# A fused spectral filter, router and expert kernel: where four groups of loads, three groups of spectra products and the narrowing of the last matrix stand in each engine's order

## The chip, the core and the metric

One Trainium2 chip, one of its cores. The metric is the device time of one launch in microseconds (us). The engines are TensorE (PE), VectorE (DVE), ScalarE (ACT), GpSimd (POOL) and SyncE (SP); each works through its own list of instructions in order and waits for the others by semaphores. SP, ACT and POOL also issue transfers.

## What is computed

The reference chains three parts. Only the batches that hold the first tokens matter in the usual case, since each expert takes the first tokens that choose it, up to a capacity.

```python
X = np.fft.rfft(x, axis=1)                      # x: 4 batches x 3072 x 256
Yr = Xr @ w_r - Xi @ w_i + b_r                  # Yi likewise; then soft threshold by 0.01
y = np.fft.irfft(Y, n=x.shape[1], axis=1)
...
logits = x @ w_gate                             # 8 experts, 384 places each, first come
h = np.maximum(np.einsum('ecd,edf->ecf', disp, w1), 0.0)
out[i] = gate_w[i] * y[expert_idx[i], pos[i]]   # y: h times w2
...
h = x @ w_in
return (h / (1.0 + np.exp(-h))) @ w_out         # 256 -> 2048 -> 256
```

## The kernel before

Large products are split into a high and a low part and done as three matmuls each (`mm3`, lines 205, 206 and 207). The transform is done as small transforms in stages. For a batch, `s1` or `first` is the first stage, `kphase` goes over 24 pairs of frequencies in steps of two (k = 0, 2, ... 22): `forward` makes `xp` (line 436) and splits it into `xk`, `shrink` makes the products `yp` with the spectral weights, 24 matmuls for a step (the "spectra products"), DVE thresholds them in three operations (lines 476 to 479), and `back` turns them back (`bp`, line 485), copies them to `bo` on ACT and stores them to DRAM as `b_d` in groups of four. The third stage is `is2`: for each of eight groups it loads rows `br` of `b_d` (two transfers, line 634), multiplies (`tiled`, line 361), copies the result to `ao` on ACT, stores it as `attn` from ACT's queue (line 640), transposes it (`tp`), copies it to `aT` on DVE and makes the logits `lg` (line 661). After four groups the logits are transposed (`lt`, line 668) and `choose` finds each token's expert on DVE.

`route` gives every token its place: a running count on DVE, matmuls `bs` (lines 695 to 698), a chain of small DVE operations, masks `pm` and `ft`, and the matmuls `tb` (line 753) that add to a table. `rank` and `slots` then read off which rows each expert takes; `gather` fetches them with indirect transfers on POOL (`xg`, three for an expert), `turn` scales them on DVE and transposes them (`gtp`, line 1064) into `xT`, and `first_ffn` runs one expert: `hp`, `hh` on ACT, `hl` on DVE (line 1087), `y`. Experts 0, 1 and 2 run first, with batch 1's third stage (`third`, line 575) and its routing beside them; then pairs of experts go through the last two matrices (`second_ffn`), which fill the last 340 us.

The two last matrices come as 64-bit floats and are narrowed on the chip. `narrow` loads a piece (`nt`), takes the absolute value on ACT (line 867), and runs four DVE operations (lines 868, 872, 873, 874); the caller then splits the result on ACT and POOL. `ffn_in` does `w_in` in eight pieces, four of them beside the first stage of batch 1 and four beside the third stage of batch 0. `ffn_out` does `w_out` in eight pieces, drawn from the loop over the experts: `n` counts that loop's steps (nine for each of experts 0, 1, 2), and at each step named in `AHEAD` one piece is written.

The order on each engine is not the order of the code. A scheduler with a timeline of its own writes each engine's list; `after(a, b)` tells it to place `a` behind `b`, without adding a wait on the chip. The tail of `kphase` for batch 1 is written behind `route`, so its products may be placed wherever the scheduler finds room; `PACE` ties some of its `xp` to steps of `is2`.

Of the kernel before, what the change touches and what calls it, by code (L numbers as in the profile page):

```python
# [26 lines left out]
QB, GT = 32, 8  # L27
# [7 lines left out]
MID = 0.5 * (P - 1)  # L35
EARLY = 3
WARM = 11
AHEAD = 4, 8, 12, 16, 20
PMS = "vav"
RING = 2  # L40
LATE = 3
PACE = {4: 2, 5: 5, **{n: GT - 1 for n in range(6, 12)}}
BIG = 65536.0
UP = 65536.0
F_MIN = UP * float(np.array(0x38000000, np.uint32).view(np.float32))
# [108 lines left out]
class Kernel:  # L154
    def __init__(self, ctx, tc, i, o):
        self.tc, self.nc, self.i, self.o = tc, tc.nc, i, o
        nc = self.nc
        cst = ctx.enter_context(tc.tile_pool(name="cst", bufs=1))
        self.dr = ctx.enter_context(tc.tile_pool(name="dr", bufs=1, space=bass.MemoryType.DRAM))
        self.zt = cst.tile([P, 1, D], F32, name="zt")  # L160
        nc.vector.memset(self.zt, 0.0)
        self.ident = cst.tile([P, P], F32, name="ident")
        make_identity(nc, self.ident)
        self.table = cst.tile([P, NF, SC * E], F32, name="table")
        self.carry = cst.tile([P, E], F32, name="carry")
        nc.gpsimd.memset(self.carry, 0.0)
        nc.gpsimd.memset(self.table, 0.0)
        self.attn = [self.dr.tile([n, D], F32, name=f"attn{h}") for h, n in enumerate((NEAR, NT - NEAR))]
        self.cst = cst
        self.tail = cst.tile([P, SC, 2, D], F32, name="tail")  # L170
        self.mixed = self.dr.tile([DFF // D, P, 3, P], F32, name="mixed")
        self.zeroed = 0
        self.stored, self.fetched, self.spread = {}, None, None
        self.again, self.away, self.evicted, self.gated = False, False, None, {}

    def spare(self, n, nm):

# [177 lines left out]
    def tiled(self, table, rows, pool):  # L355

        out = [pool.tile([P, self.CH], F32, tag="ps", name="ps1") for _ in range(2)]
        for ch in range(2):
            for p in range(2):
                at = slice(64 * p, 64 * p + N1)  # L360
                self.nc.tensor.matmul(out[p][64 * ch:64 * ch + 64], table[at, :64], rows[at, ch * self.CH:(ch + 1) * self.CH],
                                      start=True, stop=True)
        return out

    def first(self):
# [44 lines left out]
    def kphase(self, b, ads, ahead=False):  # L410

        nc, kp = self.nc, self.kp
        v = nc.vector
# [50 lines left out]
        def shrink(k, xk, xo):  # L464
            yp = self.pk.tile([P, 2, D], F32, tag="yq" if k % 4 and (b != 1 or k > 12) else "yp", name="yp", bufs=1)
            for j in range(2):
                for jj in range(2):
                    for c in range(2):
                        if jj and xo is not None and not j:
                            l = [xo[:, h, c] for h in range(2)]  # L470
                        else:
                            l = [xk[:, h, 2 * j + c, 64 - 64 * jj:192 - 64 * jj] for h in range(2)]
                        self.mm3(yp[:, j], l[0], l[1], wri[:, jj, 0, c], wri[:, jj, 1, c], jj + c == 0, jj + c == 2)
            y = self.spare(1, "y")
            bias = self.bias if xo is not None else self.bias[:, 1:2].to_broadcast([P, 2, D])
            v.tensor_tensor(y, yp, bias, ALU.add)  # L476
            cl = kp.tile([P, 2, D], F32, tag="cl", name="cl", bufs=3)
            v.tensor_scalar(cl, y, LAM, -LAM, ALU.min, ALU.max)
            self.shrunk = v.tensor_tensor(cl, y, cl, ALU.subtract).ins
            return cl  # L480
# [9 lines left out]
        x, y = {}, {}  # L490
# [122 lines left out]
    def is2(self, b, qbs, res):  # L613

        nc, bp, ps, wg = self.nc, self.bp, self.ps, self.wg
        v = nc.vector
        NB = len(qbs)  # L620
        T = QB // 2
        t0, nt = qbs[0] * T, NB * T
        bv = self.bds[b].rearrange("k (r p u g) c -> p (k r) u g c", r=2, p=2, u=4)
        r0 = b * S + t0 * 2 * TW
        h = int(r0 >= NEAR)
        od = self.attn[h][r0 - h * NEAR:r0 - h * NEAR + nt * 2 * TW].rearrange("(t p u g) d -> t p u g d", p=2, u=4, g=GT)
        res[b] = self.chosen(NB)
        GS = 4
        lgs = {}

        def rows(g):
            br = bp.tile([P, 4, D], F32, tag="xt", name="br", bufs=self.sb)
            for p in range(2):
                nc.sync.dma_start(out=br[64 * p:64 * p + N1], in_=bv[p, :, :, g])
            pt = self.tiled(self.c4, br.rearrange("q u c -> q (u c)"), ps)
            ao = bp.tile([P, 2, 2, D], F32, tag="ao", name="ao2", bufs=self.sb)
            for p in range(2):
                nc.scalar.copy(ao[:, p].rearrange("q u c -> q (u c)"), pt[p])
            for ch in range(2):
                nc.scalar.dma_start(out=od[:, :, 2 * ch:2 * ch + 2, g], in_=ao[64 * ch + t0:64 * ch + t0 + nt])  # L640
            return ao

        def turn(ao):
            aT = bp.tile([P, 2, NB, P], F32, tag="aT", name="aT")
            for h in range(2):
                tp = ps.tile([P, 4, P], F32, tag="ps", name="tp")
                for x in range(4):
                    nc.tensor.transpose(tp[:, x], ao[:, x % 2, x // 2, h * P:(h + 1) * P], self.ident)
                for ch in range(2):
                    v.tensor_copy(aT[:, h].rearrange("c b (o x t) -> c o b x t", o=2, x=4)[:, ch],  # L650
                                  tp.rearrange("c x (o b t) -> c o b x t", o=2, t=T)[:, ch, qbs[0]:qbs[0] + NB])
            return aT

        def gate(g, aT):
            z = g % GS
            if not z:
                lgs[0] = self.pk.tile([P, GS, P], F32, tag="yq", name="lg", bufs=1)
            lg = lgs[0]
            for h in range(2):
                for j in range(NB):  # L660
                    self.gated[g] = nc.tensor.matmul(lg[COL * j:COL * (j + 1), z], wg[:, h], aT[:, h, j], start=h == 0, stop=h == 1).ins
            if z == GS - 1:
                n = COL * NB
                ls = self.spare(2, "ls").rearrange("p a (b c) -> p (a b) c", b=2)
                nc.scalar.copy(ls[:n], lg[:n])
                lt = ps.tile([P, GS, NB, COL], F32, tag="ps", name="lt")
                for y in range(GS):
                    nc.tensor.transpose(lt[:, y].rearrange("p b e -> p (b e)"), ls[:n, y], self.ident[:n, :n])
                self.choose(lt.rearrange("p g b e -> p b g e")[:, :, :, :E], res[b], slice(g + 1 - GS, g + 1))

        ao, aT = {}, {}
        for g in range(GT + 2):
            if g < GT:
                ao[g] = rows(g)
            if 0 < g <= GT:
                aT[g - 1] = turn(ao.pop(g - 1))
            if g > 1:
                gate(g - 2, aT.pop(g - 2))
            yield

    def route(self, b, qbs, res):
# [13 lines left out]
        nc.tensor.matmul(bs[:, 0], tri, last, start=True, stop=NB == 1)  # L695
        for j in range(1, NB):
            nc.tensor.matmul(bs[:, 0, :, j:], ones, last[:, :, :NB - j], start=False, stop=j == NB - 1)
        nc.tensor.matmul(bs[:, 1], ones, last, start=True, stop=True)
        v.tensor_tensor(inc, inc, oh, ALU.mult)
        ex = bp.tile([P, NC, 1], F32, tag="ex", name="ex", bufs=1)  # L700
        nc.gpsimd.tensor_scalar(ex, m2.rearrange("p b g o -> p (b g) o"), -1.0 * STEP, E * STEP - MID, ALU.mult, ALU.add)
# [31 lines left out]
        for j in range(NB):  # L733
# [16 lines left out]
                        self.after(here.ins, prev.ins)  # L750
                        self.made = here.ins
            for t in range(GT):
                nc.tensor.matmul(tb, pm[:, t], ft[:, j * GT + t], start=(j + t == 0), stop=(j * GT + t == NC - 1))
        for j in range(NB):
            v.tensor_tensor(self.carry, self.carry, bs[:, 1, :, j], ALU.add)
        v.tensor_tensor(self.table, self.table, tb, ALU.add)
# [96 lines left out]
    def narrow(self, src, n, after):  # L853
# [5 lines left out]
        t = pool.tile([P, n, 2], I32, tag="nt", name="nt", bufs=3)  # L859
        for sv, dv in src:  # L860
            ins = nc.sync.dma_start(out=t[:, dv], in_=sv.bitcast(I32).rearrange("p (n z) -> p n z", z=2))
            self.after(ins.ins, self.fetched)
        low, high = t[:, :, 0], t[:, :, 1].bitcast(F32)
        a = pool.tile([P, n], F32, tag="na", name="na")
        u = a.bitcast(I32)
# [147 lines left out]
    def weights(self, s, later=0):  # L1013
# [11 lines left out]
        def quarter(z, behind=None):  # L1025
            for m, sv in enumerate((v1[:, :, z * D:(z + 1) * D], v2[:, 2 * z:2 * z + 2])):
                st = self.mq.tile([P, 2, D], F32, tag="st", name="st", bufs=4)
                nc.sync.dma_start(out=st, in_=sv)
                w = self.mq.tile([P, 2, 2, D], FR, tag=f"w{m}", name=f"w{m}")
                self.hi("a", w[:, 0], st)  # L1030
                if behind:
                    self.after(self.lastact.ins, behind)
                self.lo("p" if m and s < EARLY and not self.again else "v", w[:, 1], st, w[:, 0])
                out[m].append(w)

        for z in range(4 - later):
# [287 lines left out]
```

## Time and profile before

| | |
|---|---|
| device time, median of 3 runs | 625.69 us (625.66 to 627.39) |
| the profiled execution | 631.12 us, span 629.3 us, mean granted clock 0.985 |
| busy in the span | PE 604.0 us (96%), DVE 420.3, ACT 340.0, POOL 202.5 |

The profiled execution is 5.4 us longer than the median. PE is busy nearly all the time, so the table says little about where time can be won. What helps is a list of the places where PE waits, and of the stretches in which its granted clock is below 1.00. From about 285 us on, the two kernels' lists are the same work in the same order; only a branch that isn't taken differs.

### The profile page before, as it was taken

What the parts mean: (1) busy time and instruction counts of PE and PEld (TensorE: products, weight loads), DVE (VectorE), ACT (ScalarE), POOL (GpSimd) and SP (SyncE); (2) the same over time, 40 slices, a digit from 0 to 9 for tenths busy, and PEclk for the clock granted to TensorE, in tenths of its full rate; (3) what the DMA queues carried; (4) which work ended last, traced back from release to release, by engine and by line L of the source; (5) the groups of instructions that cost most, each with busy time, mean ns of one, the idle gap of its engine ahead of it and who ended that gap; (6) DMA issues with size and microseconds to landing.
All of it is one profiled execution on the core that took longest, in us unless ns stands there. A gap on an engine that the chain in (4) does not pass through costs nothing.

```text
span 629.3 us, 11503 instructions
## 1 busy us (share of the span) xinstructions
PE 604.0 (96%) x4128; PEld 562.8 (89%) x4128; DVE 420.3 (67%) x837; ACT 340.0 (54%) x722; POOL 202.5 (32%) x196
## 2 busy tenths in 40 slices
PE   9999999899989999899999999999999999999993
PEld 9888898567987688789999999999999999999993
DVE  2454878635973689889886687576577577485552
ACT  2535656344533556257775566556567555475561
POOL 1000113300044334254754503445403443163433
PEclk9999999999997999799999999999999999999998
DMA  8638867983446688610453543413433130010001
GB/s 205 195 98 248 286 212 236 266 232 86 168 145 215 185 255 269 204 51 26 131 179 119 157 137 110 153 33 118 142 125 110 50 126 24 14 63 27 15 2 55
DMA packets 66011, 86.09 MB, mean 137 GB/s; under 512 B 6068, under 2 KB 55864, under 8 KB 65944
## 3 DMA queue, kind: packets, MB, share of 16 engines
q1 hardware_dynamic: 53976, 69.53, 36.4%
q10 hardware_dynamic: 9664, 9.44, 4.8%
q0 software_dynamic: 2304, 6.29, 3.2%
q8 instruction: 34, 0.56, 0.4%
q14 instruction: 33, 0.27, 0.1%
HBM read 54.31 MB, written 30.93 MB: 135 GB/s over the span
## 4 chain that ended last, share of the span: by engine, by line
PE 85%; DMA 5%; DVE 5%; issue 2%; POOL 1%; ACT 1%; SPq 1%; POOLq 0%; DVEq 0%
PE o L206 7%; PE o L207 7%; PE o L205 7%; PE h L205 6%; PE h L206 6%; PE h L207 6%; PE hp L205 3%; PE hp L206 3%; PE hp L207 3%; PE y L207 3%; PE y L205 3%; PE y L206 3%; PE xp L436 3%; PE yp L205 3%; PE yp L207 3%; PE yp L206 3%
## 5 line engine op out<-in xcount | busy, mean ns | idle before, releaser
L1219 DVE TENSOR_TENSOR u<-h,u 128x384 f32<-128x384 f32 x224 | 117.6, 552 | 58.5 <-PE h L207 52.5
L1157 ACT ACTIVATE u<-u 128x384 f32<-128x384 f32 x128 | 64.2, 522 | 73.3 <-DVE u L1219 72.7
L206 PE MATMUL o<-wo,gl 128*128 128x256 f32 x369 | 99.8, 282 | 0.6 <-DVE gl L197 0.6
L207 PE MATMUL o<-wo,gh 128*128 128x256 f32 x369 | 99.8, 282 | 0.0
L205 PE MATMUL o<-wo,gh 128*128 128x256 f32 x369 | 88.0, 282 | 0.1
L197 POOL TENSOR_TENSOR ring<-mt,ring 128x384 fp32r<-128x384 f32 x32 | 37.9, 1184 | 135.7 <-ACT ring L189 135.7
L197 POOL TENSOR_TENSOR gl<-u,gh 128x384 fp32r<-128x384 f32 x62 | 65.1, 1067 | 29.1 <-ACT gh L189 26.4
L206 PEld LDWEIGHTS o<-wo,gl 128*128 128x128 f32 x369 | 69.7, 189 | 1.2 <-DVE gl L197 0.9
L207 PEld LDWEIGHTS o<-wo,gh 128*128 128x128 f32 x369 | 69.6, 189 | 0.0
L205 PEld LDWEIGHTS o<-wo,gh 128*128 128x128 f32 x369 | 65.3, 189 | 0.4 <-ACT gh L189 0.4
L189 ACT CAST gh<-u 128x384 fp32r<-128x384 f32 x126 | 63.2, 510 | 3.3 <-PE o L207 1.6
L1086 ACT ACTIVATE hh<-hp 128x384 fp32r<-128x384 f32 x64 | 31.4, 490 | 51.7 <-PE y L206 24.4
L1087 DVE SCALAR_TENSOR_TENSOR hl<-hp,hh 128x384 fp32r<-128x384 f32 x64 | 35.2, 554 | 33.2 <-ACT hh L1086 28.9
L205 PE MATMUL yp<-wri,xk 128*128 128x256 f32 x188 | 56.1, 298 | 0.9 <-DVE tail L476 0.9
L206 PE MATMUL yp<-wri,xk 128*128 128x256 f32 x188 | 53.9, 287 | 0.0
L207 PE MATMUL yp<-wri,xk 128*128 128x256 f32 x188 | 53.7, 286 | 0.0
L197 DVE TENSOR_TENSOR w<-st,w 128x512 fp32r<-128x512 f32 x52 | 38.1, 743 | 18.9 <-ACT w L189 18.1
L189 ACT CAST w<-st 128x512 fp32r<-128x512 f32 x64 | 38.7, 620 | 17.6 <-DMA st<-in_moe_w 9.1
L205 PE MATMUL hp<-xT,w 128*128 128x384 f32 x128 | 45.1, 353 | 1.5 <-DVE xT L197 1.5
L206 PE MATMUL hp<-xT,w 128*128 128x384 f32 x128 | 44.5, 347 | 0.0
L207 PE MATMUL hp<-xT,w 128*128 128x384 f32 x128 | 43.9, 345 | 0.0
L205 PE MATMUL y<-hh,w 128*128 128x384 f32 x128 | 43.9, 343 | 0.0
(254 smaller groups left out, 1512.0 us busy)
## 6 DMA issues: line engine op xcount, KB each, us to landing
st<-in_moe_w SPq DMA_DIRECT2D x64, 256.0 KB, 3.0
out<-zt SPq DMA_DIRECT2D x48, 256.0 KB, 3.4
b_d<-bo ACTq DMA_DIRECT2D x12, 512.0 KB, 4.1
mt<-mixed SPq DMA_DIRECT2D x32, 192.0 KB, 2.3
xt<-in_x SPq DMA_DIRECT2D x15, 384.0 KB, 7.0
nt<-in_moe_w_in SPq DMA_DIRECT2D x8, 512.0 KB, 5.2
nt<-in_moe_w_out SPq DMA_DIRECT2D x16, 256.0 KB, 5.3
a_d<-ao SPq DMA_DIRECT2D x8, 384.0 KB, 3.8
```

The source lines that it names most:

```text
L189: self.lastact = self.nc.scalar.copy(dst, src)
L197: return e.tensor_tensor(dst, src, raw(hi), ALU.subtract).ins
L205: first = nc.tensor.matmul(out, lh, rh, start=start, stop=False)
L206: nc.tensor.matmul(out, ll, rh, start=False, stop=False)
L207: return first.ins, nc.tensor.matmul(out, lh, rl, start=False, stop=stop).ins
L436: return [nc.tensor.matmul(xp[:, c], ar[:, kq, c * P:(c + 1) * P], c2[:, tb], start=True, stop=True).ins for c in range(2)]
L1086: self.rectified = nc.scalar.activation(hh, hp, AF.Relu).ins
L1087: self.evicted = nc.vector.scalar_tensor_tensor(hl, hp, 0.0, raw(hh), ALU.max, ALU.subtract).ins
L1157: act.activation(sg, sg, AF.Silu)
L1219: v.tensor_tensor(to, h, u, ALU.add)
```

## The change

Five edits. `narrow` places its loads behind the first matmul of the first `tiled` (`begun`) instead of behind the last load of the spectrum. The first products `yp` of steps k = 10, 14 and 18 of batch 1 are placed behind the last `lt`, `bs` and `tb` of the routing (`HOLD`). `AHEAD` names steps 2, 5, 8, 11 and 14 instead of 4, 8, 12, 16 and 20. The first low part of expert 0's second weight goes to DVE instead of POOL.

```diff
-AHEAD = 4, 8, 12, 16, 20
+AHEAD = 2, 5, 8, 11, 14
...
+HOLD = {10: "lt", 14: "bs", 18: "tb"}
...
-                self.nc.tensor.matmul(out[p][64 * ch:64 * ch + 64], table[at, :64], rows[at, ch * self.CH:(ch + 1) * self.CH],
-                                      start=True, stop=True)
+                ins = self.nc.tensor.matmul(out[p][64 * ch:64 * ch + 64], table[at, :64], rows[at, ch * self.CH:(ch + 1) * self.CH],
+                                            start=True, stop=True).ins
+                self.begun = self.begun or ins
...
+                        if b == 1 and k in HOLD and not jj and not c:
+                            self.after(ins, self.held[HOLD[k]])
...
-            self.after(ins.ins, self.fetched)
+            self.after(ins.ins, self.begun or self.fetched)
...
-                self.lo("p" if m and s < EARLY and not self.again else "v", w[:, 1], st, w[:, 0])
+                self.lo("p" if m and 0 < s + z and s < EARLY and not self.again else "v", w[:, 1], st, w[:, 0])
```

On SP, at the end of batch 0's spectrum, the list before is as follows (`nt` are the narrowing's loads of `w_in`, `ar` rows of batch 1, `br` the rows of the third stage):

```order
L861 DMA nt_1196<-in_moe2_w_in 128x1024
L861 DMA nt_1259<-in_moe2_w_in 128x1024
L420 DMA ar_1671<-a_d1_428 128x4x256
L861 DMA nt_1349<-in_moe2_w_in 128x1024
L861 DMA nt_1381<-in_moe2_w_in 128x1024
L420 DMA ar_1761<-a_d1_428 128x4x256
L909 DMA mixed_74<-mt_1270 128x2x384
L634 DMA br_1047<-b_d0_233 48x4x256 x2
L634 DMA br_1061<-b_d0_233 48x4x256 x2
L634 DMA br_1090<-b_d0_233 48x4x256 x2
```

The list of the change at the same place:

```order
L422 DMA ar_1671<-a_d1_428 128x4x256
L422 DMA ar_1761<-a_d1_428 128x4x256
L638 DMA br_1047<-b_d0_233 48x4x256 x2
L638 DMA br_1061<-b_d0_233 48x4x256 x2
L638 DMA br_1090<-b_d0_233 48x4x256 x2
L866 DMA nt_1196<-in_moe2_w_in 128x1024
L866 DMA nt_1259<-in_moe2_w_in 128x1024
L638 DMA br_1126<-b_d0_233 48x4x256 x2
L638 DMA br_1161<-b_d0_233 48x4x256 x2
L866 DMA nt_1349<-in_moe2_w_in 128x1024
L866 DMA nt_1381<-in_moe2_w_in 128x1024
L638 DMA br_1207<-b_d0_233 48x4x256 x2
```

The four loads have moved from ahead of the first `br` to behind the sixth and the tenth. On ACT the narrowing moves with them; the change has this at the start of the third stage (`ps1` is the result of the first matmuls, `na` the narrowing):

```order
L642 COPY ao2_1056<-ps1_1050 128x512
L190 COPY bo_1666<-bp_1712 128x512
L872 ACTIVATE na_1198<-nt_1196 128x512
L492 DMA b_d1_1019<-bo_1666 128x4x256
L642 COPY ao2_1056<-ps1_1051 128x512
L642 COPY ao2_1070<-ps1_1064 128x512
L644 DMA attn0_71<-ao2_1056 96x2x256 x2
L190 CAST wi_86<-na_1198 128x2x128
L872 ACTIVATE na_1261<-nt_1259 128x512
L190 CAST wi_86<-mt_1270 128x2x128
L642 COPY ao2_1070<-ps1_1065 128x512
```

A narrowing now stands between the two halves of one group's copy. On PE, at batch 0's routing, the list before has these rows; products `yp` are shown by the first row of a step and of what comes next (1817 is step k = 12, then 14, 16, 18, 20):

```order
L668 MATMUL lt_1407<-ident_62,tail_73 128x96 x4
...
L205 MATMUL yp_1817<-wri_228,xk_1763 128x256
...
L205 MATMUL yp_1863<-wri_228,xk_1807 128x256
...
L695 MATMUL bs_1425<-inc_1423,rt_1039 128x24
...
L205 MATMUL yp_1907<-wri_228,xk_1853 128x256
...
L205 MATMUL yp_1953<-wri_228,xk_1897 128x256
...
L205 MATMUL yp_1997<-wri_228,xk_1943 128x256
L753 MATMUL tb_1459<-ft_1453,pm_1460 128x72 x8
L753 MATMUL tb_1459<-ft_1453,pm_1470 128x72 x8
L753 MATMUL tb_1459<-ft_1453,pm_1488 128x72 x8
L206 MATMUL yp_1997<-wri_228,xk_1943 128x256
```

And the change:

```order
L672 MATMUL lt_1407<-ident_62,tail_73 128x96 x4
L206 MATMUL yp_1773<-wri_228,xk_1717 128x256
...
L700 MATMUL bs_1425<-inc_1423,rt_1039 128x24
...
L206 MATMUL yp_1817<-wri_228,xk_1763 128x256
...
L206 MATMUL yp_1907<-wri_228,xk_1853 128x256
...
L758 MATMUL tb_1459<-ft_1453,pm_1460 128x72 x8
L758 MATMUL tb_1459<-ft_1453,pm_1470 128x72 x8
L758 MATMUL tb_1459<-ft_1453,pm_1488 128x72 x8
...
L206 MATMUL yp_1953<-wri_228,xk_1897 128x256
...
L206 MATMUL yp_1997<-wri_228,xk_1943 128x256
```

Before, `tb` stands behind all but 47 of the 288 product matmuls of batch 1; now 72 are behind it. Between the last `lt` and `bs` there were 46, now 24. On DVE, at the end of expert 1, the list before mixes the fifth narrowing (`na_2946`, `nsg_3190`) with the sums of a pair of experts (`tm`, `yf`):

```order
L1087 SCALAR_TENSOR_TENSOR hl_2934<-hp_2926,hh_2933 128x384
L868 TENSOR_SCALAR na_2946<-na_2946 128x512
L1115 TENSOR_TENSOR tm_3071<-yf_2910,yf_2588 128x384
L873 SCALAR_TENSOR_TENSOR na_2946<-na_2946,nsg_2949 128x512
L1116 TENSOR_TENSOR tm_3072<-yf_2910,tm_3071 128x384
L699 TENSOR_TENSOR inc_2665<-inc_2665,oh_2185 128x64
L712 SCALAR_TENSOR_TENSOR base_2683<-bs_2667,carry_68 128x8
L1118 TENSOR_TENSOR yf_2910<-yf_2910 128x384
L874 SCALAR_TENSOR_TENSOR na_2946<-nt_2943,na_2946 128x512
L872 TENSOR_SCALAR nsg_3190<-nt_3184 128x512
L1121 TENSOR_TENSOR yf_2588<-yf_2588,tm_3072 128x384
L703 TENSOR_REDUCE pos_2673<-inc_2665 128x8
```

In the change the same stretch is:

```order
L1092 SCALAR_TENSOR_TENSOR hl_2946<-hp_2938,hh_2945 128x384
L1120 TENSOR_TENSOR tm_3071<-yf_2922,yf_2600 128x384
L696 SCALAR_TENSOR_TENSOR inc_2677<-smask_1036,oh_2185 128x64
L712 RECIPROCAL gt_2689<-sm_2187 128x8
L1121 TENSOR_TENSOR tm_3072<-yf_2922,tm_3071 128x384
L1123 TENSOR_TENSOR yf_2922<-yf_2922 128x384
L192 CAST gh_2691<-gt_2689 128x8
L1126 TENSOR_TENSOR yf_2600<-yf_2600,tm_3072 128x384
L198 TENSOR_TENSOR gl_2692<-gt_2689,gh_2691 128x8
L1092 SCALAR_TENSOR_TENSOR hl_2963<-hp_2955,hh_2962 128x384
```

The three operations of the fifth narrowing and the first (`nsg_3190`) of the sixth are gone from here; the fifth is now written at step 14 of the loop over the experts, where it was at step 20.

## Rows read from the trace of the kernel before

**Rows 1.** PE's waits, 80 to 300 us: us in total, times, longest.
```profile
PE gtp L1064 <- DVE xg L1057: 3.3, 2, 1.9
PE y L207 <- DVE hl L1087: 2.9, 1, 2.9
PE ps L361 <- DMA br<-b_d: 2.2, 1, 2.2
PE hp L205 <- DVE xT L197: 1.5, 1, 1.5
PE yp L205 <- DVE tail L476: 0.9, 1, 0.9
```

**Rows 2.** Four stretches: busy time of each engine, PE's clock, DMA share, GB/s.
```profile
193.03:251.24 58.21, 56.44 (x321) 46.38 (x320) 39.78 (x80) 32.52 (x65) 21.27 (x19) 0.96 0.75 228
116.18:150.10 33.92, 33.92 (x281) 21.12 (x281) 15.30 (x46) 13.56 (x26) 2.15 (x2) 1.00 0.77 211
190.67:197.08 6.41, 6.22 (x18) 5.49 (x19) 1.75 (x4) 1.45 (x3) 3.00 (x3) 0.50 0.60 193
258.60:265.20 6.60, 5.89 (x18) 5.89 (x19) 5.56 (x20) 0.98 (x2) 0.00 (x0) 0.50 0.83 261
```

**Rows 3.** The chain that ended last: start, us, piece.
```profile
86.71 0.87 PE bp L485 x4
...
105.56 7.43 DMA b_d<-bo
...
113.06 2.98 DMA br<-b_d
...
197.37 2.59 PE pw L1069 x12
```

**Rows 4.** SP's queue at the start of the third stage: start, us.
```profile
113.06 2.81 SPq L634 DMA_DIRECT2D br<-b_d  x6
```

**Rows 5.** The page's transfers: count, KB each, median us to landing.
```profile
b_d<-bo ACTq DMA_DIRECT2D x12, 512.0 KB, 4.1
...
nt<-in_moe_w_in SPq DMA_DIRECT2D x8, 512.0 KB, 5.2
```

**Rows 6.** ACT's waits, 84 to 165 us.
```profile
ACT na L867 <- DMA nt<-in_moe_w_in: 3.3, 3, 2.4
...
ACT wi L189 <- DVE na L874: 1.6, 2, 1.4
```

**Rows 7.** ACT's timeline: a narrowing, and a copy of one tile.
```profile
96.96 0.69 ACT L867 ACTIVATE na<-nt 128x512 f32<-128x512 f32 x1 [2.40 <-DMA nt<-in_moe_w_in]
...
114.00 0.59 ACT L189 COPY bo<-bp 128x512 f32<-128x512 f32 x1 [0.51 <-PE bp L485]
```

**Rows 8.** PE's timeline: first and last of 24 product matmuls, and `tb`.
```profile
105.09 0.36 PE L205 MATMUL yp<-wri,xk 128*128 128x256 f32 x1
...
107.93 0.28 PE L207 MATMUL yp<-wri,xk 128*128 128x256 f32 x1
...
175.50 2.77 PE L753 MATMUL tb<-ft,pm 128*128 128x72 f32 x24
```

**Rows 9.** DVE's timeline: the first and the third gathered tile.
```profile
185.42 0.35 DVE L1057 TENSOR_SCALAR xg<-xg,gws 128x256 f32<-128x256 f32 x1
...
189.40 1.41 DVE L1057 TENSOR_SCALAR xg<-xg,gws 128x256 f32<-128x256 f32 x1 [0.92 <-DMA xg<-attn,srcs]
```

**Rows 10.** DVE's timeline around the narrowing beside the experts.
```profile
243.85 1.67 DVE L874 SCALAR_TENSOR_TENSOR na<-nt,na 128x512 int32<-128x512 int32 x1
...
251.71 1.06 DVE L868 TENSOR_SCALAR na<-na 128x512 f32<-128x512 f32 x1
...
253.15 0.68 DVE L873 SCALAR_TENSOR_TENSOR na<-na,nsg 128x512 int32<-128x512 int32 x1
...
254.90 0.68 DVE L874 SCALAR_TENSOR_TENSOR na<-nt,na 128x512 int32<-128x512 int32 x1
255.50 1.50 DVE L872 TENSOR_SCALAR nsg<-nt 128x512 int32<-128x512 int32 x1
...
258.71 1.01 DVE L1087 SCALAR_TENSOR_TENSOR hl<-hp,hh 128x384 fp32r<-128x384 f32 x2
```

More of the change, by code (lines that the diff above doesn't have):

```diff
@@ L173, in __init__ @@
         self.stored, self.fetched, self.spread = {}, None, None
-        self.again, self.away, self.evicted, self.gated = False, False, None, {}
+        self.again, self.away, self.evicted, self.gated, self.begun, self.held = False, False, None, {}, None, {}
     def spare(self, n, nm):
@@ L472, in shrink @@
                             l = [xk[:, h, 2 * j + c, 64 - 64 * jj:192 - 64 * jj] for h in range(2)]
-                        self.mm3(yp[:, j], l[0], l[1], wri[:, jj, 0, c], wri[:, jj, 1, c], jj + c == 0, jj + c == 2)
+                        ins = self.mm3(yp[:, j], l[0], l[1], wri[:, jj, 0, c], wri[:, jj, 1, c], jj + c == 0, jj + c == 2)[0]
+                        if b == 1 and k in HOLD and not jj and not c:
+                            self.after(ins, self.held[HOLD[k]])
             y = self.spare(1, "y")
@@ L667, in gate @@
                 for y in range(GS):
-                    nc.tensor.transpose(lt[:, y].rearrange("p b e -> p (b e)"), ls[:n, y], self.ident[:n, :n])
+                    ins = nc.tensor.transpose(lt[:, y].rearrange("p b e -> p (b e)"), ls[:n, y], self.ident[:n, :n]).ins
+                self.held["lt"] = ins
                 self.choose(lt.rearrange("p g b e -> p b g e")[:, :, :, :E], res[b], slice(g + 1 - GS, g + 1))
@@ L697, in route @@
             nc.tensor.matmul(bs[:, 0, :, j:], ones, last[:, :, :NB - j], start=False, stop=j == NB - 1)
-        nc.tensor.matmul(bs[:, 1], ones, last, start=True, stop=True)
+        self.held["bs"] = nc.tensor.matmul(bs[:, 1], ones, last, start=True, stop=True).ins
         v.tensor_tensor(inc, inc, oh, ALU.mult)
@@ L752, in route @@
             for t in range(GT):
-                nc.tensor.matmul(tb, pm[:, t], ft[:, j * GT + t], start=(j + t == 0), stop=(j * GT + t == NC - 1))
+                self.held["tb"] = nc.tensor.matmul(tb, pm[:, t], ft[:, j * GT + t], start=(j + t == 0), stop=(j * GT + t == NC - 1)).ins
         for j in range(NB):
```

## The prediction

> **What bounds the kernel now.** PE is busy 96% of the span, so its list of work sets the time, and that list is the same before and after. The change can only move the places where PE stands still or runs at a low clock. I read the views in this order. First PE's waits between 80 and 300 us [rows 1]: five lines, and behind each the engine or the transfer that ended it. Then stretches by granted clock [rows 2]: after two of the waits a stretch stands at 0.50, which is the lower of the two levels, 1.2 against 2.4 GHz. It took 6.41 us at the end of the routing and 6.60 us between experts 1 and 2. Work at half the clock takes twice as long, so half of each is lost: 3.2 and 3.3 us. That makes three places:
>
> - A, where batch 0's spectrum ends: 2.2 us for `br`, 0.9 us for `tail`, together 3.1.
> - B, behind the routing: two waits of `gtp` for gathered tiles, 3.3 us, and 3.2 of clock, together 6.5.
> - C, from expert 1 to expert 2: 1.5 for `xT`, 2.9 for `hl`, 3.3 of clock, together 7.7.
>
> So 17.3 us can be won at most, and each place is judged by what else its stretch holds.
>
> **A: the loads behind the first matmul.** The chain that ended last runs through this place [rows 3]: the store `b_d` takes 7.43 us, `br` 2.98, and then PE goes on. The page has 4.1 us as the median of such a store [rows 5]. Here `nt` loads stand ahead on SP and share the DMA engines with it. Moved behind the sixth `br`, they leave the store alone: 7.43 - 4.1 = 3.3 us sooner, more than the 2.2 waited. The narrowing's DVE work leaves the stretch too, which is what kept `tail` (0.9). I take all 3.1.
>
> It is paid in the third stage, where the four loads and narrowings now stand. SP needs 2.81 us to issue six `br` [rows 4]; then `nt` starts and lands 5.2 us later [rows 5], 8.0 behind the first `br`, while that one lands after 2.98. ACT's list has the first narrowing behind two copies only, so ACT waits some 2 us, and the second half of the first group's copy `ao` waits behind it: 0.69 for the narrowing, 0.59 for a copy [rows 7]. PE has products between the groups, but the transposes wait for `ao`. Upper bound: the four loads are 2.1 MB; the stretch moved 211 GB/s at a DMA share of 0.77 [rows 2], so 274 at a full one, and 2.1 MB take 7.7 us; ACT's waits in narrowings are 4.9 us before (3.3 + 1.6) [rows 6]. If all were passed to PE, 12.6. Lower bound nothing: the stretch from 116 to 150 has ACT busy 13.56 and DVE 15.30 of 33.92 us [rows 2], room enough for the work of four narrowings. I take 2.7, a little over half of ACT's waits, since the products that stand between the groups cover the rest, and none of the transfer time: `br` is issued several groups ahead. A nets +0.4.
>
> One rule speaks against this move. The Trainium skill says in DMA: Bandwidth & Descriptors, section "Issuing engines are not separate DMA queues", that transfers of all issuing engines land on the same 16 engines and interleave there, so that issuing from elsewhere saves only sequencer time. Here the trace agrees: `b_d`, issued from ACT, took 7.43 instead of 4.1 beside loads issued from SP. By that rule the loads would now delay `br` and `attn` in the third stage as they delayed `b_d`; that case is the last rival below.
>
> **B: products held.** `tb` now stands behind 216 of batch 1's 288 product matmuls instead of 241, and fewer stand between the last `lt` and `bs` (24, before 46). PE so reaches each step of the routing earlier in its work, and has more left for the time in which DVE, POOL and the transfers make the gathered tiles. A product costs 0.12 us (24 from 105.09 to 107.93), and `tb` ends at 178.27 [rows 8]. The first tile is ready at 185.77, 7.5 behind it, the third at 190.81, 12.5 behind it [rows 9]. PE had 47 products and two `bp` (0.87 each [rows 3]) for this: 47 x 0.12 + 2 x 0.87 = 7.4. That covers the first tile and leaves the others bare. Now it has, ahead of the first `gtp`, 49 products (5.9), six matmuls of `xp` (0.7, at half of a `bp` matmul's 0.22) and three `bp` (2.6), 9.2; then 23 products and a `bp` (3.7) ahead of the third, 12.9. The tiles come later as well, since the held steps bring DVE work between `tb` and the list of rows: I put two operations of 0.68 there [rows 10], 1.4 us. Then the first tile comes after 8.9 (no wait) and the third after 13.9, a wait of 1.0. I leave 1.8 us of the 6.5, the third tile's 1.0 and 0.8 for the second, and no fall of the clock: a gain of 4.7. The bounds are 1.5 (DVE is no faster through the routing than before, and the held products only make PE wait at `bs` and `tb`) and 6.5.
>
> **C: other steps for `w_out`.** From `hl` at 251.24 (it ends at 251.71) to the next at 258.71, DVE spends 7.0 us, of which the fifth and sixth narrowing take 1.06 + 0.68 + 0.68 + 1.50 = 3.92 [rows 10]. PE waited 2.9 of it. Without them 3.1 us remain, which is 1.0 less than PE can bear, so the wait goes, and with it the fall of the clock behind it, as nothing stops PE. The `xT` of expert 2 stood behind a narrowing operation of 1.67 [rows 10], about what PE waited for it (1.5); that piece is written earlier as well. The narrowing goes to experts 0 and 1: DVE is busy 39.78 of 58.21 us there [rows 2], and one more set of about 3.0 fits. But single operations can stand ahead of an `hl` or `xT` as those did, so I charge 1.4, the wait that one such operation made. Gain 7.7 - 1.4 = 6.3. Bounds 3.5 (each of three more pieces costs 1.4) and 7.7.
>
> **The rest.** The last `bp` of batch 1 is later in PE's list, behind twelve `hp`, and its store feeds that batch's third stage: `bo` 0.59, `b_d` 4.1, `br` 2.98 and an issue, about 8.1 us, against 12 `hp`, the `pw` (2.59 [rows 3]) and 16 `y` on PE, about 7.6 (0.18 each for 384 columns, as a product of 256 takes 0.12), a narrow margin; I charge 1.0 (0 to 2.5). PE reaches the pair sums at 274 to 284 sooner than DVE's work allows: 0.4. The low part that goes from POOL to DVE is one operation of about 0.68, hidden where DVE waits for gathers (0.92 ahead of the third tile [rows 9]); uncovered it would cost that 0.68.
>
> **Sum.** 0.4 + 4.7 + 6.3 - 1.0 - 0.4 = 10.0 us. The profiled execution has 631.12, so 621.1 there. It is 5.4 longer than the median of the runs, 625.69. Most of PE's list is the same in both, so I take the gain for both: 625.7 - 10.0 makes 615.7. Within 0.3%, 1.9 us, a measurement of this kernel can't be told from no change.
>
> **The rivals.**
> - R1, DVE is the bound in the routing. Its operations stand back to back there, and held steps add `tail` and `cl` behind the chain. B gives 1.5 and the rest stays: 10.0 - 3.2 = 6.8, with a further wait at `bs` some 5.5, so 619 to 620. Against it: `tb` is reached after fewer products.
> - R2, the 5.4 us that the profile adds lie in these very stalls. Then a plain run has 17.3 - 5.4 = 11.9 to win instead of 17.3, and 10.0 - 5.4 = 4.6 are gained: 621.1. For it: the profile's long operations (1.67 and 1.50 beside 0.68 for the same shape) look like disturbed ones; against it: waits for transfers don't depend on them.
> - R3, the narrowing moves its stall into experts 0 and 1. C gives nothing (each piece stalls an `hl` once, one with a fall of the clock): 10.0 - 6.3 = 3.7, 622.0. For it: DVE is at 68% there; against it: PE has two chains to switch between until batch 1's third stage ends.
> - R4, slower: the third stage starves. The loads share DMA engines with `br` and `attn` at a share that is already 0.77 [rows 2]. All of the 12.6 above are paid, and behind one or two long waits the clock falls as at B and C, 3.3 each. The other terms give 10.0 - 0.4 + 3.1 = 12.7; so the stage must lose over 12.7 before the whole is slower. At 12.6 + 2 x 3.3 = 19.2 the time is 632. Against it: `br` is issued ahead, and ACT has over half of the stretch free.
> - R5, the change does little: the held rows only reorder work that PE would have found anyhow, C gains what A loses. Within 1.9 of 625.7.
>
> **How the numbers follow.** My forecast has 0.48, its own range 612 to 619.5: a gain of 13.7 if A pays nothing (2.7 more) and C's charge falls away by 1.0, of 6.2 if A pays half of its upper bound (6.3 in place of 2.7, 3.6 less). R1 0.16, R2 0.12, R3 0.08, R4 0.10, R5 0.06. The range from 610.5 (every term near its better bound) to 623.5 takes in R1 to R3, 0.84 in all. Faster: 0.48 + 0.16 + 0.12 + 0.08 = 0.84; slower 0.10; same 0.06.
>
> **What the profile after would show.** A: PE's wait for `br` at the first L361 is gone or under 0.5 us; ACT waits for `nt` inside the third stage, and PE for `ao` or `aT`, 2 to 3 us in all. B: the waits of `gtp` under 2 us in sum, and clock 1.00 behind them. C: no wait of `y` for `hl` of more than 1 us at expert 2, and clock 1.00 from 240 to 270. If PE waits for `br` or `aT` over 5 us between 112 and 150, or its clock falls there, R4 is at work; a new wait at `bs` or `tb` is R1; waits of `hl` at 200 to 245 are R3. The prediction is wrong above all if the transfers of the third stage pay more than the 2.7 that I put there.

## The result, and the profile after

The changed kernel takes 634.67 us in the median of six runs (630.70 to 636.71), the kernel before 625.95 us (624.60 to 627.39): a ratio of 1.014, 95% interval [1.0114, 1.0167]. It is slower by 8.7 us, where 10 us less were forecast.

PE's waits after, from 80 to 300 us of the profiled execution (us in total, times, longest); they answer to [rows 1]:

```profile
PE ps L579 <- DMA br<-b_d: 4.1, 1, 4.1
PE gtp L1069 <- DVE xg L1062: 2.5, 4, 0.8
PE tp L652 <- ACT ao L642: 0.9, 1, 0.9
...
PE y L208 <- DVE hl L1092: 0.5, 1, 0.5
```

Three of the waits named beforehand are gone: `br` at the first matmul of batch 0's third stage (2.2), `xT` (1.5) and the long `hl` (2.9). In their place stands one of 4.1 us at L579, the first matmul of batch 1's third stage, which was 0.3 us before. Summed up, PE's waits are 11.7 us, against 12.8 in the first profile of before and 9.1 in a second one (below). So the waits tell only a part of it; the granted clock adds to them. Four stretches of the same execution, busy times as in [rows 2]:

```profile
118.00:132.00 14.00, 12.83 (x82) 7.10 (x84) 13.48 (x30) 7.99 (x17) 3.02 (x4) 0.88 1.07 309
203.00:213.00 10.00, 6.95 (x20) 4.72 (x22) 2.25 (x4) 1.93 (x4) 1.98 (x2) 0.66 0.62 170
206.00:213.00 7.00, 6.95 (x20) 4.72 (x22) 1.29 (x3) 1.00 (x2) 0.00 (x0) 0.51 0.56 166
245.00:255.00 10.00, 7.68 (x39) 5.68 (x38) 6.96 (x9) 4.00 (x10) 3.83 (x3) 0.83 0.77 233
```

The second stretch takes in the last 3 us of the wait of 4.1 us, which ends at 206.05. The third shows what follows the wait: from 206 to 213 PE works at the lower level for nearly the whole time (0.51), which costs it 3.4 us (7 x 0.49). The fourth is behind three waits for gathered tiles, at 0.83. The first, in batch 0's third stage, is at 0.88, but the kernel before, profiled again, has 0.89 there, so this fall isn't shown to be the change's:

```profile
118.00:132.00 14.00, 14.00 (x93) 7.53 (x91) 4.12 (x11) 4.85 (x9) 1.19 (x1) 0.89 0.92 253
```

The chain of waits for the first rows (start, us, piece):

```profile
195.03 4.60 DMA b_d<-bo
199.71 6.29 DMA br<-b_d
206.05 1.92 PE ps L579 x4
```

The store took 4.60, about the 4.1 that the forecast used; the rows took 6.29 in place of 2.98. The four matmuls behind them took 1.92, against 1.05 in the run with the rows placed first (below).

**Where PE loses time.** To compare executions, each row of PE's timeline is given the median time that one of its kind takes in all the traces of this study; what the span has used beyond the sum of these is lost, whether by a wait or by the clock. In us, by stretch (the kernels of the last three columns come below):

| stretch | before, first profile | before, again | change | held products | held, bp first | change, bp first |
|---|---|---|---|---|---|---|
| 90 to 150 | 7.1 | 8.2 | 9.4 | 6.4 | 6.7 | 9.9 |
| 180 to 200 | 7.6 | 5.1 | 2.8 | 4.4 | 3.4 | 3.5 |
| 200 to 235 | 1.8 | 2.0 | 9.7 | 5.7 | 2.5 | 2.2 |
| 235 to 265 | 8.1 | 3.1 | 6.2 | 9.2 | 2.7 | 5.2 |
| start to 290 | 31.3 | 23.2 | 33.5 | 32.0 | 21.5 | 23.8 |

One execution of a kernel differs from the next by some us, and the entries move by 1 us and more with the way in which rows are grouped, so a column places a loss; its size is taken from the medians of the timed runs. Against the second profile of before, the change loses 7.7 us more from 200 to 235 and 3.1 more from 235 to 265.

### The profile page after: what moved, and what is told of

Same layout as the page of the kernel before. It is cut to its first block, busy times and chain, and to the rows that moved or that the text cites. A ratio compares the mean times of both kernels' runs of the same rounds, so it can differ in the third digit from the quotient of the medians.

```text
span 632.5 us, 11519 instructions
## 1 busy us (share of the span) xinstructions
PE 608.1 (96%) x4128; PEld 561.0 (89%) x4128; DVE 421.7 (67%) x838; ACT 338.3 (53%) x722; POOL 197.3 (31%) x195
## 3 DMA queue, kind: packets, MB, share of 16 engines
q0 software_dynamic: 2304, 6.29, 3.1%
## 4 chain that ended last, share of the span: by engine, by line
PE 85%; DMA 5%; DVE 4%; issue 2%; ACT 1%; SPq 1%; POOL 0%; POOLq 0%; DVEq 0%; ACTq 0%
PE o L207 7%; PE o L208 7%; PE o L206 7%; PE h L206 6%; PE h L207 6%; PE h L208 6%; PE hp L206 4%; PE hp L207 3%; PE hp L208 3%; PE y L208 3%; PE xp L438 3%; PE y L206 3%; PE y L207 3%; PE yp L207 3%; PE yp L206 3%; PE yp L208 3%
## 5 line engine op out<-in xcount | busy, mean ns | idle before, releaser
L198 POOL TENSOR_TENSOR wi<-na,wi 128x256 fp32r<-128x256 f32 (+1 forms) x8 | 9.1, 1140 | 120.3 <-ACT wi L190 120.3
L206 PE MATMUL hp<-xT,w 128*128 128x384 f32 x128 | 44.8, 351 | 0.0
L207 PE MATMUL hp<-xT,w 128*128 128x384 f32 x128 | 44.0, 344 | 0.1
```

The costliest lines, as they stand in the source:

```text
L198: return e.tensor_tensor(dst, src, raw(hi), ALU.subtract).ins
L206: first = nc.tensor.matmul(out, lh, rh, start=start, stop=False)
L207: nc.tensor.matmul(out, ll, rh, start=False, stop=False)
```

## The experiments

The four parts of the change (loads, held products, steps, low part) are taken one at a time, then all but one, then with one more edit. Each was compared with runs of the kernel before on the same chip.

**The kernel before, once more.** Its first profile had 631.12 us.

> The kernel before, unchanged, profiled again, because its first profiled execution took 631.12 us and its median is 626. Theory 1: the 5 us more lie in PE's waits and stretches of clock 0.50 between 180 and 265 us; a usual execution (about 626) has 5 us less of them, so there was less to win than the 17.3 us of the forecast. Rival: the 5 us are spread over the span or lie behind 290 us, and the stalls A, B and C are as long as in the first profile (4.9, 7.6 and 7.7 us lost by PE).

It took 624.96 us. PE's waits from 80 to 300 us:

```profile
PE gtp L1064 <- issue: 2.1, 1, 2.1
PE yp L205 <- DVE tail L476: 1.4, 1, 1.4
PE ps L361 <- DMA br<-b_d: 1.1, 1, 1.1
PE hp L205 <- DVE xT L197: 1.0, 1, 1.0
PE y L207 <- DVE hl L1087: 0.8, 1, 0.8
```

And its stretch at expert 2:

```profile
245.00:255.00 10.00, 9.54 (x56) 9.45 (x56) 9.81 (x26) 6.87 (x15) 3.75 (x5) 1.00 0.97 327
```

The wait for `hl` is 0.8, not 2.9, and no fall of the clock follows it: from 235 to 265 us PE loses 3.1, not 8.1. So 5.0 of the extra time of the first profile lay at C and 2.5 at B. Theory 1 holds; the forecast had priced one execution's stall as the kernel's.

**One part alone.** Kernels with one part of the diff each (the line that acts is shown, cut at its end in the last), the rest as before:

```diff
e1  +            self.after(ins.ins, self.begun or self.fetched)
e2  +HOLD = {10: "lt", 14: "bs", 18: "tb"}
e3  +AHEAD = 2, 5, 8, 11, 14
e7  +                self.lo("p" if m and 0 < s + z and s < EARLY and not self.again else "v", ...)
```

> The kernel before with the loads of w_in held behind the first matmul of the third stage, and nothing else of the change. Theory 1: PE loses about 2.3 us more between 90 and 135 us (7.2 in place of 4.9, as in the profile of the change), 628 to 629 us in all. Rival: these loads are the main cause of the loss, since all that ACT and DVE have to do comes later from then on: 632 us or more. The forecast's own term says 625.5.

> The kernel before with the products held behind the three steps of the routing, and nothing else. Theory 1: the waits for the gathered tiles fall by about 4 to 5 us, and the third stage of batch 1 waits for its first rows instead, with a stretch of clock at half behind it, about 8 us: 628 to 630 us, with a wait of 3 to 5 us of the first matmul of that stage. Rival: the wait there comes from the loads that stand ahead on SP (the narrowing of w_out at other steps), not from the holding: then no such wait here, and 621 us.

> The kernel before with the pieces of w_out written at steps 2, 5, 8, 11 and 14, and nothing else. Theory 1: the wait for hl at expert 2 is gone, but another takes its place at the gathered tiles of expert 2, whose scaling on DVE runs beside splits on POOL and takes 1.2 us for a tile in place of 0.35: 624 to 628 us. The forecast's own term: the whole stall of 7.7 us less 1.4, 619 to 620. Rival: the earlier loads delay br on SP, and the first matmul of batch 1's third stage waits 3 us or more: 629 us or more.

> The kernel before with the first low part of expert 0's second weight on DVE in place of POOL, and nothing else. Theory 1 and the forecast: hidden, 624 to 626 us. Rival: it is on DVE's list ahead of the gathered tiles' scaling and costs 0.7 us and more, with a longer wait of gtp behind it: 626 to 627.

| part | median, us | ratio, 95% interval | against before's median of the same runs |
|---|---|---|---|
| loads behind the first matmul | 628.17 | 1.005 [1.0031, 1.0069] | +3.2 |
| products held | 633.03 | 1.013 [1.0099, 1.0161] | +8.1 |
| steps of w_out | 621.00 | 0.9929 [0.9902, 0.9956] | -4.0 |
| low part on DVE | 622.90 | 0.9977 [0.9955, 0.9998] | -2.1 |

Holding is the main loser, and the loads lose too; the steps gain, and so does the low part, which the forecast priced at nothing, though its interval nearly reaches no change (0.1 to 2.8 us). The loads came out as theory 1 has it. The three others didn't: the held products cost more than the 628 to 630 expected, with a wait of 1.9 us in place of 3 to 5; the steps lie below theory 1's range and above the forecast's own; the low part lies below both of its ranges. The held products alone show the wait at L579 without the other parts, so it isn't owed to the loads on SP alone:

```profile
PE y L206 <- ACT hh L1091: 2.8, 3, 1.1
PE ps L579 <- DMA br<-b_d: 1.9, 1, 1.9
PE gtp L1069 <- DVE xg L1062: 1.6, 3, 1.0
```

Its two lost stretches:

```profile
203.00:213.00 10.00, 10.00 (x45) 6.10 (x41) 6.67 (x11) 3.81 (x7) 3.62 (x3) 0.83 0.53 158
245.00:255.00 10.00, 7.13 (x30) 6.25 (x30) 8.12 (x21) 5.92 (x12) 3.16 (x4) 0.84 0.78 241
```

**What the low part does.** Third gathered tile of expert 0, DVE's timeline of the kernel before, profiled again:

```profile
190.01 1.66 DVE L1057 TENSOR_SCALAR xg<-xg,gws 128x256 f32<-128x256 f32 x1 [0.33 <-issue]
```

POOL's timeline of the same execution:

```profile
190.24 1.27 POOL L197 TENSOR_TENSOR w<-st,w 128x512 fp32r<-128x512 f32 x1
```

And DVE with the low part moved:

```profile
188.64 0.35 DVE L1062 TENSOR_SCALAR xg<-xg,gws 128x256 f32<-128x256 f32 x1 [0.64 <-DMA xg<-attn,srcs]
```

The same operation takes 0.35 us alone and 1.66 while POOL's split runs; it ends 0.16 us behind that one (191.67 and 191.51). So the third tile came 1.3 us late because of what POOL did, and this edit takes that away. The `1.41` of [rows 9] was the same thing. How this becomes 2.1 us isn't shown: from the second tile's transposes to the first `hp` PE takes 4.0 us in the one profile (189.40 to 193.41) and 3.6 in the other (187.72 to 191.30), and the rest of the second's lead is there ahead of the first tile.

**The last `bp` first.** Held products alone, with one more order:

```diff
-                    self.mm3(hp, w[:, 0, h, c], w[:, 1, h, c], xT[:, 0, h], xT[:, 1, h], h == 0, h == 1)
+                    ins = self.mm3(hp, w[:, 0, h, c], w[:, 1, h, c], xT[:, 0, h], xT[:, 1, h], h == 0, h == 1)[0]
+                    if not e and not j and not h and not self.again:
+                        self.after(ins, self.backed)
```

> The products held as in the change (nothing else of it), with the first hp of expert 0 placed behind the last bp of batch 1, so that this bp is no longer behind twelve hp. Theory 1: holding costs its 8 us because the last spectrum of batch 1 is stored later, so that its third stage, and what SP and ACT have queued behind that, come late; with bp first again, the first matmul of that stage waits under 1 us and the time is 621 to 626 us. Rival: holding costs by itself, through the DVE and ACT work that the held steps push behind the routing (the splits of expert weights, hh, xT): 630 us or more, with waits for hh and xT at 235 to 255 us as before.

It took 623.01 us (0.9978 [0.9963, 0.9994]), 10.0 less than without this order. Three of its waits:

```profile
PE hp L206 <- DVE xT L198: 0.8, 1, 0.8
PE gtp L1069 <- issue: 0.8, 2, 0.5
PE ps L579 <- DMA br<-b_d: 0.8, 1, 0.8
```

And the same stretches:

```profile
203.00:213.00 10.00, 10.00 (x54) 7.19 (x51) 6.77 (x12) 4.99 (x9) 4.43 (x4) 1.00 0.68 203
245.00:255.00 10.00, 9.22 (x55) 8.90 (x54) 9.81 (x29) 5.92 (x12) 4.00 (x5) 1.00 0.89 284
```

One order of one matmul brings back both stretches, the clock with them, and theory 1 holds. The twelve `hp` now stand between this `bp` and L579, so PE reaches L579 at nearly the same time in both kernels (200.76, without the order 200.58); the store is issued at 192.65 in place of 194.51. By the table, 3.2 of the 10.0 us lie from 200 to 235 and 6.5 from 235 to 265. The same order in the whole change:

> The whole change, with the first hp of expert 0 placed behind the last bp of batch 1, as in the run that took 623.0 us. Theory 1 (the loss of the change is the late store of that batch's spectrum, plus the 3.2 us of the loads): 634.7 falls by 8 to 12 us, to 622 to 626, and the wait of 4.1 us at the first matmul of batch 1's third stage is under 1 us. Rival: with the loads and the earlier pieces of w_out present as well, SP's queue keeps that stage late whatever PE does: 629 us or more.

624.74 us (0.9982 [0.9965, 0.9999]), 9.9 less than the change. No `br` wait over 0.2 is left at L579; the loads' stretch, 90 to 150 us, loses 9.9, about what it loses in the change (9.4). Here 7.5 us lie from 200 to 235 and 1.0 from 235 to 265.

**Rows ahead of w_out.** The whole change, in which the loads of the fourth `w_out` piece stood on SP at 197.55, ahead of the rows at 199.71, with them placed behind the rows:

```diff
+            if self.row0 and self.late:
+                self.after(ins.ins, self.row0)
```

> The whole change, with the one piece of w_out whose two loads stood ahead of the first rows of batch 1's third stage placed behind the first two loads of rows. If these loads lengthen the rows' way (6.29 us in place of some 3.5), the wait of 4.1 us at that stage's first matmul falls to 1 to 2 us, and the time by 3 to 6 us, to 629 to 632. Rival: the rows are late because their store is late, whatever stands ahead on SP: 633 to 636 us.

630.84 us (1.0093 [1.0058, 1.0129]), 3.8 less. The chain there:

```profile
196.45 4.24 DMA b_d<-bo
200.82 4.35 DMA br<-b_d
```

The rows take 4.35 in place of 6.29, and the wait is 2.7 in place of 4.1, not the 1 to 2 expected; the time is in the range expected, though its interval overlaps the change's a little. In the change without the new steps (next), where no such loads stand there, the rows take 3.65. So these loads, which have time to spare, do lengthen the rows' way when they stand ahead.

**The steps, the stores and what adds up.**

> The change with the pieces of w_out at the old steps. If parts add up (loads 3.2, held products 8.1, low part -2.1): 634 us, no better than the whole change, whose earlier pieces then gain nothing. If the earlier pieces deepen the wait of batch 1's third stage: 630 us or less, and a wait there of 2 us or less.

> The held products alone (633.0 us), with the stores of batch 1's third stage issued from ACT in place of SP. If the loads of weights and of w_out come late because SP stands at these stores, ACT's waits for them at 230 to 260 us (6.0 us in sum) fall below 3 us and the time is 628 to 631 us. Rival: issuing costs ACT as much as SP's queue cost, or the loads are late for another reason: 632 us or more.

The change without the new steps took 635.63 us (1.0161 [1.012, 1.0202]): beside the late store, the steps gain 1 us, which the intervals don't tell from nothing, in place of the 4.0 that they gain alone; the 3.8 of the loads ahead of the rows fit that. With the stores of batch 1's third stage on ACT (`nc.scalar.dma_start` in place of `nc.sync.dma_start` at L586), the held products took 633.96 (1.013 [1.0092, 1.0168]), no better, and the waits at L579 rose to 6.9 us in two (5.0 the longer). ACT's waits for loads from 230 to 262 us are gone there, but one of 4.4 us for the stores stands in their place. That the second loss, at 235 to 260 us, comes through SP's queue is not shown by this. ACT's waits in the held kernel from 230 to 260 us say only that loads were late there, 6.0 us in two places, where the run with `bp` first has 0.9 in one:

```profile
ACT w L190 <- DMA st<-in_moe_w: 3.6, 1, 3.6
ACT na L872 <- DMA nt<-in_moe_w_out: 2.4, 1, 2.4
```

**What the loads cost.** A kernel that was to keep the loads where they were and to move the work of the narrowing:

```diff
-        nc.scalar.activation(a, high, AF.Abs, scale=UP)
+        ab = nc.scalar.activation(a, high, AF.Abs, scale=UP)
+        if self.begun:
+            self.after(ab.ins, self.begun)
```

> The kernel before with the loads of w_in where they were, but the first ACT operation of each narrowing that is written later placed behind the first matmul of the third stage (so the work moves as in the change and the transfers don't). Theory 1: most of what the loads' move costs (3.2 us, 628.2 in place of 625.0) is ACT standing in its order at the narrowing until the load lands (3.4 us in the profile of the change): with the loads early that wait is gone and the time is 624.5 to 626. Rival: the work itself between the groups' copies costs it: 627.5 to 629.

624.81 us (1.0003 [0.9982, 1.0024]), 3.4 less than with the loads moved, which is in theory 1's range. But the edit held only two of the four loads. The kernel before issues them at 91.91 and 102.00, two each; in this one the second two went behind eight `br`:

```profile
91.27 1.53 SPq L866 DMA_DIRECT2D nt<-in_moe_w_in  x2
...
114.87 1.21 SPq L866 DMA_DIRECT2D nt<-in_moe_w_in  x2
```

So it doesn't part the transfers' place from the work's. It shows that the work and two of the loads can move without a cost in the median, and that the 3.2 us are there when the first two loads move as well. ACT's waits for these loads are 5.9 us in it, against 3.4 in the change, and its one profile, 627.12 us and near the top of its runs (621.99 to 627.63), loses 10.3 us from 90 to 150, no less than the change. Why the loads cost 3.2 us stays open. In the change, ACT's timeline at the stage's start is:

```profile
117.23 0.67 ACT L872 ACTIVATE na<-nt 128x512 f32<-128x512 f32 x1 [3.39 <-DMA nt<-in_moe_w_in]
...
117.79 1.07 ACT L642 COPY ao<-ps 128x512 f32<-128x512 f32 x2
```

ACT stands 3.39 us at the narrowing, and the copies that PE's transposes need are behind it; PE's wait for them is 0.9 in sum, beside 0.6 for `aT`.

**Without a part, and versions for use.**

> The change without the held products. If the parts add up as measured alone (loads 3.2, steps -4.0, low part -2.1): 622 us. Rival: loads and steps get in each other's way, since the w_out pieces follow the w_in pieces on SP and in the narrowing's buffers: 625 us or more.

> The kernel before with two parts of the change: the steps 2, 5, 8, 11 and 14 and the low part on DVE. Adding up: 619 us (625.0 - 4.0 - 2.1). Rival: both take time from the same stall, the fall of the clock behind the gathered tiles, and only the larger counts: 621 us.

> The change without the moved loads and with the first hp behind the last bp. Adding up: 617 to 619 us, the fastest here (621.3 without the low part, which alone gave 2.1). Rival: the held products have already taken the wait at the third gathered tile, which is what the low part shortens, so nothing is added: 621 to 622 us.

> The same, with the pieces of w_out at steps 2, 5, 8, 11 and 14 as well. Theory 1: what the steps alone gave (4 us) and what holding gives at the gathered tiles add up: 616 to 621 us. Rival: 626 us or more, since the loads of w_out stand ahead of the rows of batch 1's third stage on SP.

| kernel | median, us | ratio, 95% interval |
|---|---|---|
| change without the held products | 623.47 | 0.9952 [0.9934, 0.9970] |
| steps and low part | 621.16 | 0.9924 [0.9897, 0.9950] |
| steps, low part, held products, `bp` first | 623.25 | 0.9954 [0.9936, 0.9973] |
| steps, held products, `bp` first | 621.27 | 0.9946 [0.9931, 0.9961] |

The gains don't add up: steps (4.0), low part (2.1) and held products with `bp` first (2.0) would make 8 together, and all three end at 2.6 below the kernel before, the two mixes of two parts at 3.8 and 4.7. Without the held products the change ends between what adding up and the rival give. Steps and low part came out at their rival's 621, though which stall they share isn't shown; the three parts together are slower than either of their ranges, and steps and held products with `bp` first lie 0.3 above theirs. The steps alone, and the steps with the low part, have the lowest ratios of the study, 0.7 to 0.8% below the kernel before; these two and the steps with the held products aren't told apart.

## Why the prediction was wrong

**The rest: the step that failed.** It saw that the last `bp` goes behind twelve `hp` and that the margin is narrow, and charged "1.0 (0 to 2.5)". Measured, this order is worth 10.0 us alone and 9.9 in the change. PE's way was put at 7.6 us, and that was right: in the held kernel PE goes from the end of that `bp` at 193.10 to L579 at 200.58 in 7.5 us, in the change in 8.3 (193.61 to 201.95). The way of the spectrum, put at 8.1, was sized too short: it took 9.4 in the held kernel (until 202.45) and 12.4 in the change (until 206.00). The rows of the held kernel, PE and ACT and then the chain:

```profile
192.08 1.02 PE L489 MATMUL bp<-cl,c 128*128 128x256 f32 x4
...
192.49 1.13 ACT L190 CAST w<-st 128x512 fp32r<-128x512 f32 x2
193.52 0.49 ACT L1091 ACTIVATE hh<-hp 128x384 fp32r<-128x384 f32 x1
193.90 0.59 ACT L190 COPY bo<-bp 128x512 f32<-128x512 f32 x1
...
194.51 4.07 DMA b_d<-bo
198.66 3.79 DMA br<-b_d
```

The held `bp` came when ACT had splits and an `hh` on its list, so `bo` began 0.8 us behind it. The rows took 3.79, and 6.29 in the change, in place of 2.98: the loads of `w_out` ahead of them were looked at for DVE's time, not for SP's order. And the clock was counted at B and C and not here, though a wait stands ahead of it here too: it cost 3.4 us behind the 4.1 waited in the change and 1.7 behind the 1.9 of the held kernel. In the change this place holds 7.5 of the 9.9 us. What stays open is why a second loss follows at 235 to 260 us, which is the larger one in the held kernel (6.5 of 10.0); that it goes with the same order is shown, the way there isn't.

**A** was put at +0.4 net; alone it costs 3.2. The 3.1 that it should give were given (both waits are gone), and the payment was 2.7 by forecast, some 6 by the run (3.1 + 3.2), within its bounds of 0 to 12.6. The waits that were to make it are there but small: 1.5 us for `ao` and `aT` in the profile of the change, where 2 to 3 were forecast. What makes up the rest isn't shown.

**B** was put at 4.7. From 180 to 200 us the change loses 2.8, 4.8 less than the first profile, close to the forecast for that execution; the waits for these tiles are 0.2 there, where 1.8 were left in the sum, and the clock is 1.00. But a usual one loses 5.1, and holding with the `bp` in its place gives 2.0 in time.

**C** was put at 6.3; the steps give 4.0. The long `hl` wait and the clock behind it stood in one execution only. The operation of 1.50 us that the forecast put down to the narrowing takes 0.41 in the second profile; it was stretched beside a split of POOL (last section). And the clock that was to be 1.00 from 240 to 270 is at 0.83 from 245 to 255 in the change, behind gathered tiles that were not in the sum. The rival that the profile's extra 5.4 us lie in these stalls was right, and it was given 0.12; two profiles of the kernel before, had they been there, would have shown it.

**The low part** was put at nothing and gives 2.1 (0.1 to 2.8). The forecast read the 1.41 us of [rows 9] as a long row, and POOL's split beside it as cover.

**Of the rivals**, R4 named the mechanism (loads that share the way with rows, a long wait, the clock behind it) and a time of 632, but put it in batch 0's third stage, where PE loses 9.4 against 8.2 and 7.1 in the two profiles of before; it happened in batch 1's. One of R4's signs, a fall of the clock from 112 to 150, is in the change's profile, and in the second of before too. Together: the parts alone sum to 3.2 + 8.1 - 4.0 - 2.1 = 5.2, and the whole is 8.7 slower; the loads ahead of the rows, 3.8, which need the late store and the new steps both, fit the difference.

The rule of the Trainium skill that was weighed against the change, in DMA: Bandwidth & Descriptors, section "Issuing engines are not separate DMA queues", is borne out for the store: with the loads gone from beside it, `b_d` from ACT takes 3.66 us in the change, in place of 7.43 [rows 3]:

```profile
104.11 3.66 DMA b_d<-bo
```

The second place where the change puts loads beside rows wasn't looked at. There both come from SP, so 6.29 us for rows behind loads, and 4.35 ahead of them, show that loads share the rows' way, and nothing about the issuing engine.

## What to carry to other kernels

When an edit puts work behind a point in one engine's order, follow what that work produces to its next reader, and price a narrow margin there with all that it depends on: the copy's place in ACT's list, whatever else stands in the reader's queue, and PE's clock behind the wait. A stall that is to be won should be seen in two executions first, since here 5 of 8 us of one were in one profile only. Read the list that an edit makes before its time is read: here a kernel that was to keep four loads in place had moved two. Hold a group of edits apart by parts before judging it: two of these four gain, and the one order that the held products lacked was worth 10 us.

## What the runs showed of the hardware that was not expected

A DVE operation that runs beside one of POOL can take as long as POOL's, and longer: the scaling of a tile takes 0.35 us alone and 1.66 beside a split of 1.27. In the change the same comes at expert 2, where three splits of POOL stand in a row:

```profile
246.15 1.28 POOL L198 TENSOR_TENSOR w<-st,w 128x512 fp32r<-128x512 f32 x1 [5.86 <-DMA attn<-ao]
247.38 1.32 POOL L198 TENSOR_TENSOR wo<-na,wo 128x512 fp32r<-128x512 f32 x1
248.66 1.31 POOL L198 TENSOR_TENSOR w<-st,w 128x512 fp32r<-128x512 f32 x1
```

DVE's first tile there:

```profile
246.23 1.35 DVE L1062 TENSOR_SCALAR xg<-xg,gws 128x256 f32<-128x256 f32 x1
```

Its three tiles take 3.89 us together, 1.3 each, and PE's three waits for them sum to 2.3. The Trainium skill says in SBUF — State Buffer, section "Who interferes with whom", that DVE and GpSimd share one pair of ports under an exclusive lock; these rows agree with it.

Which of the two engines is held up differs from one execution to the next. From expert 1 to expert 2, the kernel before has in its first profile, beside the `nsg` of 1.50 in [rows 10]:

```profile
255.42 1.30 POOL L197 TENSOR_TENSOR w<-st,w 128x512 fp32r<-128x512 f32 x1 [2.94 <-ACT w L189]
256.69 1.44 POOL L197 TENSOR_TENSOR wo<-na,wo 128x512 fp32r<-128x512 f32 x1
...
256.93 1.61 DVE L1121 TENSOR_TENSOR yf<-yf,tm 128x384 f32<-128x384 f32 x1
```

In its second profile the same places are:

```profile
254.28 2.10 POOL L197 TENSOR_TENSOR w<-st,w 128x512 fp32r<-128x512 f32 x1 [2.94 <-ACT w L189]
...
254.37 0.41 DVE L872 TENSOR_SCALAR nsg<-nt 128x512 int32<-128x512 int32 x1
254.70 0.54 DVE L1121 TENSOR_TENSOR yf<-yf,tm 128x384 f32<-128x384 f32 x1
```

There POOL's split is the long one. The two DVE rows differ by 2.2 us in sum, and the wait for the `hl` behind them by 2.1 (2.9 and 0.8). So much of the stall at C was of this kind; no run here takes the splits away from that place alone.

The clock fell behind a short wait in one kernel and not in others, at the same place: in the held kernel, behind 1.9 us of standing still, 203 to 213 is at 0.83 in the mean, which is another 1.7 us (10 x 0.17). With the stores on ACT a wait of 1.9 us, and in the change without the new steps one of 2.4, was followed by 1.00 there. So the length of the wait alone doesn't decide it.
